# Moving the loads of v: by pairs of chunks instead of by pairs of heads, and onto GpSimd's queue

## The chip, the cores and the metric

The kernel runs on one NeuronCore of a Trainium2 chip, as one launch. The metric is the device time of one execution, in microseconds (us). Three runs of the kernel before gave 1208.64, 1209.57 and 1211.05 us, a median of 1209.57 us.

## The reference, cut to what matters

Three stages follow each other, all in float32 at their edges:

```python
# 1. attention inside chunks of 64 tokens; q, k, v are [8 batches, 8 heads, 576, 64]
scores = (q_c @ k_c.T) / 8           # per batch, head, chunk: 64 x 64
attn   = softmax(scores)
x      = (attn @ v_c)                # -> x [4608 tokens, 512]
# 2. mixture of experts: logits = x @ w_gate; tokens assigned greedily by logit,
#    at most 576 for each of 8 experts; out = relu(x @ w1[e]) @ w2[e]
# 3. h = max(x @ m1, x @ m2, x @ m3);  result = h @ m_out     [4608, 512]
```

The change touches only the loads of stage 1.

## The kernel before, in words

Attention takes the first 165 us or so of the execution. Its work is cut into nine units of 8 chunks with all 8 heads, and each unit into four groups of 2 chunks (128 tokens), 36 groups in all. `ORDER` (line 37) says what a unit is: units 0 to 3 and 5 to 8 are eight consecutive chunks of one batch; unit 4 (`None`) collects the one remaining chunk of each of the eight batches.

For a unit there are three tensors to load, 1 MB each. `load_qk` (line 52) brings q and k into a tile of 128 partitions; one DMA of 512 KB brings four heads of a whole unit in runs of 1 KB. In unit 4 every chunk comes from another batch, so there it is eight DMAs of 128 KB, each into 16 partitions; those of chunks 4 to 7 are issued by GpSimd, the others by SyncE. `load_v` (line 65) brings v into one of three buffers `VB` (`vb_93`, `vb_94`, `vb_95` in the listings below), in runs of 256 bytes. In a usual unit, part n of four holds the head pair n for all eight chunks: two DMAs of 128 KB into 64 partitions each. The first half (s = 0) is issued by SyncE, the second by GpSimd; in unit 0 both by SyncE. In unit 4 a part holds two chunks with all heads, as four DMAs of 64 KB.

The loop over groups (line 245) issues in step i the loads of coming units: of q and k one half of the heads of one of the two tensors for the unit after next (`load_qk`, unit i//4 + 2), of v part i%4 for the next unit (`load_v`, unit i//4 + 1). SyncE first issues a tiny DMA of the maxima of group i-1 (`tick`, line 249), and so its loads of step i don't start before that group's maxima exist. Then, for group i: `scores` on TensorE into the PSUM tile pS, `smax` and `ssub` on VectorE, `expo` on ScalarE. For group i-1: `att_t` transposes the weights, and `pv` multiplies by v (line 181, into pX). `pv` of a group reads chunks 2h and 2h+1 of its unit with all four head pairs in turn, 4 matmul rows for each pair. For group i-2: `scale` (line 185) divides by the row sums on VectorE and writes the tile X, and GpSimd sends X to DRAM (`xd`, line 190). X has three buffers (`bufs=3`, line 187): `scale` of group g overwrites that of group g-3, and waits until the `xd` DMA of group g-3 has landed. The transposes of q and k for the next unit (`trans`, line 105) run in the same step.

All engines run their instructions in the order in which the program issues them. DMAs signal completion through semaphores. Eight of them serve the DMAs of GpSimd in turn (DMASW0 to DMASW7) and eight those of SyncE and ScalarE (DMAHW0 to DMAHW7): the n-th DMA of a kind waits for the landing of the (n-8)-th of that kind before it is issued. So at most eight of a kind are under way.

Before the loop, SyncE issues the loads of q and k for unit 0, half of unit 1, all of v for unit 0, and the rest of unit 1. GpSimd clears two of the buffers of v (lines 91 and 92), then builds some 30 constants for the later routing stage (`consts()`, line 94), and only then comes to its part of the loop.

Of the kernel before, what the change touches and what calls it, by code (L numbers as in the profile page):

```python
# [17 lines left out]
B, H, S, D = 8, 8, 576, 64  # L18
# [10 lines left out]
def attention(ctx, tc, q, k, v, wg_in, xd, L, ident, consts, early, tick, mark):  # L29

    nc = tc.nc
# [5 lines left out]
    ORDER = [0, 1, 2, 3, None, 4, 5, 6, 7]  # L37

    def chunk(u, j):

        b = ORDER[u]
        return (b, b % 2 + j) if b is not None else (j, 0 if j % 2 else 8)
# [9 lines left out]
    def load_qk(nm, u, h, n):  # L52

        if h == 0:
            QK[nm, u] = P.tile([128, H, 4 * D], F32, name="in" + nm)
        src = k if nm == "k" else q
        m = 8 if ORDER[u] is not None else 1
        for j in range(0, 8, m):
            b, c = chunk(u, j)
            (nc.gpsimd if j >= 4 else nc.sync).dma_start(  # L60
                QK[nm, u][16 * j:16 * (j + m), h:h + n],
                bass.AP(tensor=src.tensor, offset=src.offset + (b * H + h) * S * D + c * 64 * D,
                        ap=[[4 * D, 16 * m], [S * D, n], [1, 4 * D]]))

    def load_v(u, part):

        t = VB[u % 3]
        if ORDER[u] is not None:
            b, c = chunk(u, 0)
            for s in range(2):  # L70
                (nc.gpsimd if u and s else nc.sync).dma_start(
                    t[s * 64:(s + 1) * 64, :, part, s, :],
                    bass.AP(tensor=v.tensor, offset=v.offset + (b * H + 2 * part + s) * S * D + c * 64 * D,
                            ap=[[D, 64], [64 * D, 8], [1, D]]))
            return
        for j in (2 * part, 2 * part + 1):
            b, c = chunk(u, j)
            for s in range(2):
                (nc.gpsimd if u and s else nc.sync).dma_start(
                    t[s * 64:(s + 1) * 64, j, :, s, :],  # L80
                    bass.AP(tensor=v.tensor, offset=v.offset + b * H * S * D + s * S * D + c * 64 * D,
                            ap=[[D, 64], [2 * S * D, 4], [1, D]]))

    for h in (0, 4):
        for nm in "kq":
            load_qk(nm, 0, h, 4)
# [3 lines left out]
    for t, eng in ((VB[0], nc.vector), (VB[1], nc.gpsimd), (VB[2], nc.gpsimd)):  # L90
        eng.memset(t[0:64, :, :, 1, :], 0.0)
        eng.memset(t[64:128, :, :, 0, :], 0.0)
    nc.scalar.dma_start(wg[:, :, :8], wg_in.rearrange("(a p) e -> p a e", p=128))
    consts()
    warm = PS.tile([128, 4, 128], F32, name="pA", bufs=1)
    for i in range(14):
        nc.tensor.transpose(warm[:, i % 4, :], ident, ident)
    for nm in "kq":
        load_qk(nm, 1, 0, 4)
    for n in range(4):  # L100
        load_v(0, n)
    for nm in "kq":
        load_qk(nm, 1, 4, 4)

# [140 lines left out]
    for i in range(G):  # L245
        u, n = i // 4 + 1, i % 4
# [6 lines left out]
        if tr:  # L253
            load_v(u, n)
# [440 lines left out]
def kernel(ctx, tc, q, k, v, w_gate, w1, w2, m1, m2, m3, m_out, out, mark=lambda n: None):  # L695
# [10 lines left out]
    with ExitStack() as c2:  # L706
        consts = c2.enter_context(tc.tile_pool(name="tmp", bufs=1))
        rt.unit(consts)
        attention(c2, tc, q, k, v, w_gate, xd, rt.L, rt.ident, lambda: rt.consts(consts), rt.early, tick, mark)
# [579 lines left out]
```

## Time and profile before

| quantity | value |
|---|---|
| median of 3 runs | 1209.57 us (1208.64 to 1211.05) |
| profiled execution, its own time | 1214.07 us |
| span in its profile | 1212.3 us |
| TensorE busy | 1175.5 us, 97% of the span |
| VectorE / ScalarE / GpSimd busy | 68% / 34% / 25% |
| mean granted TensorE clock | 0.985 of full speed |
| DMA | 242.99 MB, 200 GB/s on the mean |

The span runs from the first to the last instruction; the execution's own time lies 1.8 us above it. Of the page's 40 slices of 30 us the first two, the first 60 us of attention, show TensorE busy for 7 and 8 tenths, the next three for 9 tenths or more, and the DMA engines at 9 tenths or more through the first four. In the rows below, "idle" times in square brackets name what ended them; a share of DMA above 1 means that packets overlap on an engine.

### The profile page before, as it was taken

How to read it: one execution, taken by the hardware profiler on the slowest of the kernel's cores; microseconds unless marked ns; L12 is line 12 of the kernel's file. 1: busy time of each engine (PE TensorE's matmuls, PEld its weight loads, DVE VectorE, ACT ScalarE, POOL GpSimd, SP SyncE). 2: the span in 40 equal slices, each digit the busy share in tenths (PEclk: the TensorE clock that was granted, in tenths of full speed). 3: DMA queues.
4: the chain of work that ended last, by engine and by line, in shares of the span. 5: the costliest groups of instructions: out<-in, count | busy, mean ns of one | idle time of the engine just before them, and what ended most of it. 6: DMA issues, size and time to landing. Idle time of an engine off the chain costs nothing.

```text
span 1212.3 us, 23567 instructions
## 1 busy us (share of the span) xinstructions
PE 1175.5 (97%) x9508; PEld 1098.6 (91%) x9508; DVE 829.2 (68%) x1652; ACT 413.7 (34%) x674; POOL 306.8 (25%) x507
## 2 busy tenths in 40 slices
PE   7899978999999999999999999999999999999998
PEld 6788856999999999998999998998998998998996
DVE  6788976877788888787843565565565565565561
ACT  5788822333333242334432113113113113113111
POOL 7433201010027465745970002002002002002002
PEclk9999978999999999999999999999999999999999
DMA  9999615273556556567654763663763763773651
GB/s 260 246 262 263 175 54 165 89 239 116 187 171 196 190 200 215 172 226 250 222 195 181 270 243 139 269 247 136 270 250 135 270 258 128 274 258 121 230 193 52
DMA packets 138828, 242.99 MB, mean 200 GB/s; under 512 B 30048, under 2 KB 101216, under 8 KB 131808
## 3 DMA queue, kind: packets, MB, share of 16 engines
q1 hardware_dynamic: 118608, 180.90, 45.4%
q0 software_dynamic: 14976, 51.13, 12.5%
q10 hardware_dynamic: 5136, 9.46, 2.1%
q8 instruction: 75, 1.23, 0.4%
q14 instruction: 33, 0.27, 0.1%
HBM read 195.05 MB, written 46.40 MB: 199 GB/s over the span
## 4 chain that ended last, share of the span: by engine, by line
PE 50%; issue 36%; DVE 6%; DMA 4%; POOL 3%; SPq 1%; ACT 1%; POOLq 1%; DVEq 0%; ACTq 0%
PE acc L1099 16%; PE acc L1044 13%; PE pX L181 2%; PE py L1137 2%; POOL out_dram L1221 2%; PE po L1213 2%; PE pT L115 2%; PE px L1137 2%; PE pz L1137 2%; DMA inq<-in_q_dram 2%; PE pS L132 1%; PE pA L168 1%; PE pxt L816 1%; DVE chunk L763 1%; DMA vb<-in_v_dram 1%
## 5 line engine op out<-in xcount | busy, mean ns | idle before, releaser
L1044 PE MATMUL acc<-xhi,chunk 128*128 128x288 f32 (+2 forms) x1024 | 208.1, 302 | 4.8 <-DVE hlo L1077 4.1
L1099 PE MATMUL acc<-hhi,chunk 128*128 128x288 f32 x1024 | 209.9, 299 | 1.3 <-DVE hlo L1077 1.3
L1044 PEld LDWEIGHTS acc<-xhi,chunk 128*128 128x128 f32 x1024 | 161.6, 189 | 6.8 <-DVE hlo L1077 5.0
L1221 POOL DMA_INDIRECT out_dram<-ot,ia x36 | 36.4, 1012 | 516.3 <-ACT ot L1219 515.7
L1099 PEld LDWEIGHTS acc<-hhi,chunk 128*128 128x128 f32 x1024 | 162.9, 188 | 1.9 <-DVE hlo L1077 1.5
L1099 PE MATMUL acc<-hlo,chunk 128*128 128x288 f32 x512 | 150.8, 294 | 0.0
L1213 PE MATMUL po<-chunk,h 128*128 128x512 f32 x648 | 149.3, 390 | 0.0
L1213 PEld LDWEIGHTS po<-chunk,h 128*128 128x128 f32 x648 | 121.5, 188 | 24.8
L1044 PE MATMUL acc<-xlo,chunk 128*128 128x288 f32 (+2 forms) x512 | 143.8, 296 | 0.0
L1137 PE MATMUL px<-xb,wa 128*128 128x384 f32 x648 | 129.9, 334 | 0.7 <-ACT ys L1106 0.7
L1137 PE MATMUL py<-xt,wb 128*128 128x384 f32 x648 | 129.8, 334 | 0.0
L1137 PEld LDWEIGHTS px<-xb,wa 128*128 128x128 f32 x648 | 113.9, 188 | 1.4 <-ACT ys L1106 1.0
L1137 PEld LDWEIGHTS py<-xt,wb 128*128 128x128 f32 x648 | 114.0, 188 | 0.5
L1158 ACT CAST h<-best 128x384 fp32r<-128x384 f32 x72 | 37.0, 514 | 198.1 <-DVE best L1156 121.3
L1099 PEld LDWEIGHTS acc<-hlo,chunk 128*128 128x128 f32 x512 | 96.0, 188 | 0.0
L763 DVE TENSOR_TENSOR chunk<-raw,chunk 128x1024 fp32r<-128x1024 f32 x67 | 86.7, 1299 | 10.8 <-ACT chunk L756 8.0
L1044 PEld LDWEIGHTS acc<-xlo,chunk 128*128 128x128 f32 x512 | 94.1, 189 | 0.0
L1068 ACT ACTIVATE hhi<-acc 128x576 fp32r<-128x576 f32 (+1 forms) x66 | 41.9, 638 | 135.3 <-PE acc L1044 125.0
L793 POOL DMA_INDIRECT xg<-xd,idx x40 | 40.8, 1020 | 152.2 <-DVE ohe L683 75.1
L1173 ACT COPY tmp<-px 128x384 f32<-128x384 f32 x54 | 25.9, 480 | 146.2 <-PE px L1137 146.2
L756 ACT CAST chunk<-raw 128x1024 fp32r<-128x1024 f32 x67 | 69.5, 1047 | 11.3 <-ACT ys L1106 6.0
L1077 DVE SCALAR_TENSOR_TENSOR hlo<-acc,hhi 128x576 fp32r<-128x576 f32 (+1 forms) x66 | 48.3, 735 | 33.0 <-ACT hhi L1068 32.8
(221 smaller groups left out, 2048.1 us busy)
## 6 DMA issues: line engine op xcount, KB each, us to landing
wb<-wdb SPq DMA_DIRECT2D x54, 1024.0 KB
wa<-wda SPq DMA_DIRECT2D x54, 768.0 KB
raw<-in_moe_w_dram SPq DMA_DIRECT2D x64, 512.0 KB
xd<-x POOLq DMA_DIRECT2D x36, 256.0 KB
yd<-ys ACTq DMA_DIRECT2D x32, 288.0 KB
wdb<-pair POOLq DMA_DIRECT2D x18, 512.0 KB
yraw<-yd SPq DMA_DIRECT2D x12, 768.0 KB
ink<-in_k_dram SPq DMA_DIRECT2D x16, 512.0 KB
```

Source lines behind the costliest of these rows:

```text
L756: nc.scalar.copy(hi, raw)
L763: nc.vector.tensor_tensor(lo, raw, hi.bitcast(F32), op=OP.subtract)
L793: nc.gpsimd.indirect_dma_start(out=g, out_offset=None, in_=xd[:, :], in_offset=bass.IndirectOffsetOnAxis(ap=rt.idx[r][:, t:t + 1], axis=0))
L1044: nc.tensor.matmul(acc[:, hf, :tk.stop - tk.start], w[a][:, dc, o:o + 128], x[:, dc, tk], start=n == 0, stop=n == 11)
L1068: nc.scalar.activation(hv, src, AF.Relu)
L1077: nc.vector.scalar_tensor_tensor(lv, src, 0.0, hv.bitcast(F32), op0=OP.max, op1=OP.subtract)
L1099: nc.tensor.matmul(acc[:, hf, :288], w[a][:, f, :], x[:, f, tk], start=n == 0, stop=n == 23)
L1137: nc.tensor.matmul(dst, w[:, dc, o, a], XO[x][:, c, dc], start=start and n == 0, stop=stop and n == 5, skip_group_check=True)
L1158: nc.scalar.copy(hpart(g, i, j)[0], M)
L1173: nc.scalar.copy(U[g, 1], XB[g])
L1213: nc.tensor.matmul(PO[t], h[:, x, t % 6 * 128:t % 6 * 128 + 128], w[a][:, f % 2], start=f == 0 and n == 0, stop=f == 5 and n == 2)
L1221: st = nc.gpsimd.indirect_dma_start(out=out, out_offset=bass.IndirectOffsetOnAxis(ap=ia[:, t:t + 1], axis=0), in_=ot, in_offset=None)
```

## The change: what it does

1. `load_v` loses its branch for usual units. In every unit part n now holds chunks 2n and 2n+1 with all eight heads, as four DMAs of 64 KB, each of 64 partitions by four heads. That is what group n of the unit reads.
2. All v is issued by GpSimd, except part 0 of unit 0, which SyncE issues.
3. Parts 1 to 3 of unit 0 are issued by GpSimd before `consts()`; part 0 stands where all of unit 0 stood.
4. All q and k is issued by SyncE, so the 16 small DMAs of unit 4 are no longer shared between two queues.

```diff
@@ load_qk
-            (nc.gpsimd if j >= 4 else nc.sync).dma_start(
+            nc.sync.dma_start(
                 QK[nm, u][16 * j:16 * (j + m), h:h + n],
@@ load_v
         t = VB[u % 3]
-        if ORDER[u] is not None:
-            b, c = chunk(u, 0)
-            for s in range(2):
-                (nc.gpsimd if u and s else nc.sync).dma_start(
-                    t[s * 64:(s + 1) * 64, :, part, s, :],
-                    bass.AP(tensor=v.tensor, offset=v.offset + (b * H + 2 * part + s) * S * D + c * 64 * D,
-                            ap=[[D, 64], [64 * D, 8], [1, D]]))
-            return
         for j in (2 * part, 2 * part + 1):
             b, c = chunk(u, j)
             for s in range(2):
-                (nc.gpsimd if u and s else nc.sync).dma_start(
+                (nc.gpsimd if u or part else nc.sync).dma_start(
                     t[s * 64:(s + 1) * 64, j, :, s, :],
                     bass.AP(tensor=v.tensor, offset=v.offset + b * H * S * D + s * S * D + c * 64 * D,
                             ap=[[D, 64], [2 * S * D, 4], [1, D]]))
@@ before the loop
+    for n in range(1, 4):
+        load_v(0, n)
     consts()
...
     for nm in "kq":
         load_qk(nm, 1, 0, 4)
-    for n in range(4):
-        load_v(0, n)
+    load_v(0, 0)
     for nm in "kq":
         load_qk(nm, 1, 4, 4)
```

How this moves instructions is seen in three places. The first is GpSimd's queue at the start. In the kernel before, the last constants (`free` to `wsum`) are followed by v of unit 1 (`vb_94`) and the first stores of results (`xd`):

```order
L410 MEMSET free 128x36
L412 MEMSET base 128x1
L414 MEMSET wsum 128x1
L71 DMA vb_94<-in_v_dram 64x8x64 x3
L190 DMA xd<-x 128x512
L71 DMA vb_94<-in_v_dram 64x8x64
L190 DMA xd<-x 128x512
L71 DMA vb_95<-in_v_dram 64x8x64
L190 DMA xd<-x 128x512
```

In the changed kernel (line numbers are lower by 7), 12 DMAs for unit 0 (`vb_93`) stand behind the clearing of the buffers and ahead of the constants, of which the first is `lev`:

```order
L83 MEMSET vb_95 64x32x64
L84 MEMSET vb_95 64x32x64
L71 DMA vb_93<-in_v_dram 64x4x64 x12
L356 IOTA lev 128x128
L359 IOTA i_117 128x1152
```

and behind the constants 12 DMAs, no longer three, come ahead of the first `xd`, and then four between one `xd` and the next:

```order
L403 MEMSET free 128x36
L405 MEMSET base 128x1
L407 MEMSET wsum 128x1
L71 DMA vb_94<-in_v_dram 64x4x64 x12
L183 DMA xd<-x 128x512
L71 DMA vb_94<-in_v_dram 64x4x64 x4
L183 DMA xd<-x 128x512
L71 DMA vb_95<-in_v_dram 64x4x64 x4
L183 DMA xd<-x 128x512
```

So the first `xd` moved behind 21 more DMAs than before.

The second place is the same queue with its waits, from the ninth DMA for unit 1 on, in the changed kernel (DMASW is a semaphore of GpSimd's DMAs, DVE_49 one of VectorE):

```order
L71 DMA vb_94<-in_v_dram 64x4x64 [waits DMASW4_49]
L71 DMA vb_94<-in_v_dram 64x4x64 [waits DMASW5_49]
L71 DMA vb_94<-in_v_dram 64x4x64 [waits DMASW6_49]
L71 DMA vb_94<-in_v_dram 64x4x64 [waits DMASW7_49]
L183 DMA xd<-x 128x512 [waits DMASW0_49,DVE_49]
L71 DMA vb_94<-in_v_dram 64x4x64 [waits DMASW1_49]
L71 DMA vb_94<-in_v_dram 64x4x64 [waits DMASW2_49]
L71 DMA vb_94<-in_v_dram 64x4x64 [waits DMASW3_49]
L71 DMA vb_94<-in_v_dram 64x4x64 [waits DMASW4_49]
L183 DMA xd<-x 128x512 [waits DMASW5_49,DVE_49]
```

The same stretch in the kernel before has one v DMA between two stores:

```order
L190 DMA xd<-x 128x512 [waits DVE_49]
L71 DMA vb_95<-in_v_dram 64x8x64 [waits DMASW0_49]
L190 DMA xd<-x 128x512 [waits DMASW1_49,DVE_49]
L71 DMA vb_95<-in_v_dram 64x8x64 [waits DMASW2_49]
L190 DMA xd<-x 128x512 [waits DMASW3_49,DVE_49]
```

A step of the loop is now five DMAs of GpSimd where it was two, on the same eight semaphores.

The third place is SyncE's queue in steps 8 and 9, where unit 4 is loaded. Before, with four DMAs of k in step 8 and four of q in step 9:

```order
L249 DMA tick<-mx 1x1 [waits DMAHW2_49,DMAHW0_49,DVE_49]
L60 DMA ink<-in_k_dram 16x8x256 [waits DMAHW1_49,PE_49]
L60 DMA ink<-in_k_dram 16x8x256
L60 DMA ink<-in_k_dram 16x8x256 [waits DMAHW3_49]
L60 DMA ink<-in_k_dram 16x8x256 [waits DMAHW4_49]
L71 DMA vb_93<-in_v_dram 64x8x64 [waits DMAHW5_49]
L249 DMA tick<-mx 1x1 [waits DMAHW6_49,DVE_49]
L60 DMA inq<-in_q_dram 16x8x256 [waits DMAHW7_49]
```

In the changed kernel there are eight of each, and no v between them:

```order
L242 DMA tick<-mx 1x1 [waits DMAHW0_49,DVE_49]
L60 DMA ink<-in_k_dram 16x8x256 [waits DMAHW5_49,PE_49]
L60 DMA ink<-in_k_dram 16x8x256
L60 DMA ink<-in_k_dram 16x8x256 [waits DMAHW7_49]
L60 DMA ink<-in_k_dram 16x8x256
L60 DMA ink<-in_k_dram 16x8x256 [waits DMAHW1_49]
L60 DMA ink<-in_k_dram 16x8x256 [waits DMAHW2_49]
L60 DMA ink<-in_k_dram 16x8x256 [waits DMAHW3_49]
L60 DMA ink<-in_k_dram 16x8x256 [waits DMAHW4_49]
L242 DMA tick<-mx 1x1 [waits DMAHW5_49,DVE_49]
L60 DMA inq<-in_q_dram 16x8x256 [waits DMAHW6_49]
```

All of unit 4's q and k now passes through one queue in order.

## Rows read from the trace of the kernel before

**Rows 1.** Stretches by busy time of each engine, TensorE clock, DMA share.

```profile
core 0: us, PE busy (x) PEld busy (x) DVE busy (x) ACT busy (x) POOL busy (x), PEclk, DMA share, GB/s
10.90:65.53 54.63, 45.48 (x698) 37.29 (x697) 39.58 (x76) 37.49 (x65) 25.60 (x62) 0.91 1.14 249
65.53:129.38 63.85, 63.82 (x1080) 53.15 (x1079) 56.93 (x116) 57.31 (x100) 22.39 (x36) 1.00 1.03 267
58.00:63.30 5.30, 5.29 (x52) 4.53 (x52) 2.67 (x5) 1.94 (x4) 1.27 (x2) 0.50 1.09 201
```

**Rows 2.** Timeline, TensorE: start, duration, instructions, [idle before]; first products with v.

```profile
17.06 0.88 PE L181 MATMUL pX<-vb,AT 128*64 128x128 f32 x12
20.13 0.44 PE L181 MATMUL pX<-vb,AT 128*64 128x128 f32 x4 [2.19 <-DMA vb<-in_v_dram]
```

**Rows 3.** Timeline, TensorE, groups 9 to 11.

```profile
50.87 0.69 PE L132 MATMUL pS<-kT,qT 64*64 64x64 f32 x32
...
53.39 0.88 PE L181 MATMUL pX<-vb,AT 128*64 128x128 f32 x12
58.01 0.69 PE L181 MATMUL pX<-vb,AT 128*64 128x128 f32 x4 [3.74 <-DMA inq<-in_q_dram]
58.63 1.13 PE L132 MATMUL pS<-kT,qT 64*64 64x64 f32 x32
...
65.53 0.69 PE L132 MATMUL pS<-kT,qT 64*64 64x64 f32 x32
```

**Rows 4.** Timeline, SyncE's queue: issue of loads.

```profile
5.41 9.46 SPq L71 DMA_DIRECT2D vb<-in_v_dram  x8
...
42.37 2.31 SPq L71 DMA_DIRECT2D vb<-in_v_dram  x1
...
45.63 3.93 SPq L60 DMA_DIRECT2D ink<-in_k_dram  x4
```

**Rows 5.** Timeline, GpSimd: constants, loads, stores.

```profile
9.16 0.40 POOL L363 IOTA lev<- 128x128 bf16 x1
...
19.39 2.37 POOL L71 DMA_DIRECT2D vb<-in_v_dram  x3
21.75 0.59 POOL L190 DMA_DIRECT2D xd<-x  x1
...
43.67 0.57 POOL L190 DMA_DIRECT2D xd<-x  x1 [2.35 <-DMA vb<-in_v_dram]
...
51.42 0.54 POOL L60 DMA_DIRECT2D inq<-in_q_dram  x1 [1.84 <-DMA xd<-x]
```

**Rows 6.** Timeline, GpSimd, later: small loads of v, last store, and others.

```profile
66.20 1.23 POOL L79 DMA_DIRECT2D vb<-in_v_dram  x2
...
112.18 0.71 POOL L71 DMA_DIRECT2D vb<-in_v_dram  x1
...
166.14 0.54 POOL L190 DMA_DIRECT2D xd<-x  x1 [1.43 <-DVE x L188]
169.45 0.10 POOL L953 MEMSET xg<- 128x1 f32 x1 [2.77 <-PE pT L220]
```

**Rows 7.** Timeline, VectorE: scale of group 3.

```profile
35.28 0.69 DVE L188 TENSOR_TENSOR x<-pX,rc 128x512 f32<-128x512 f32 x1
```

**Rows 8.** DMA packets of 5 to 11 us (first), 51 to 55 us.

```profile
DMA packets 2103, 2.09 MB, mean 348 GB/s; under 512 B 64, under 2 KB 2103, under 8 KB 2103
...
DMA packets 442, 0.71 MB, mean 177 GB/s; under 512 B 140, under 2 KB 317, under 8 KB 442
```

**Rows 9.** DMA queues: packets, MB, share of 16 engines; 12.5 to 16.5, 151 to 167 us.

```profile
q1 hardware_dynamic: 3028, 0.75, 140.8%
...
q0 software_dynamic: 400, 1.31, 21.3%
```

**Rows 10.** One line's instructions (shortest/median/longest ns), then VectorE's timeline.

```profile
L158 DVE TENSOR_SCALAR sm<-sm x36: 140/171/678, 18.8 to 164.0; 128x8 f32<-128x8 f32 x36
...
112.57 0.32 DVE L158 TENSOR_SCALAR sm<-sm 128x8 f32<-128x8 f32 x1
```

## The prediction

> **What bounds the kernel now.** I read the stretches of the attention stage first. From the scores of group 0 at 10.90 us to those of group 11 at 65.53 us TensorE is busy for 45.48 of 54.63 us; from there to 129.38 us it is busy for 63.82 of 63.85 us [rows 1]. The second stretch holds 16 groups, so a group costs 63.85 / 16 = 3.99 us where TensorE never waits. The first holds 11 groups and would take 43.9 us at that pace: 10.7 us are lost, and the change can win back those 10.7 us and hardly more, as later groups wait for no load. In both stretches the DMA share is about 1 or above, so loads are the suspect.
>
> TensorE's timeline shows where. At 17.06 us the product of group 0 with v does 12 of its 16 rows and then idles 2.19 us for v [rows 2]. At 53.39 us group 8, the first of unit 2, again does 12 rows, idles 3.74 us and ends at 58.7 us [rows 3]. Twelve rows are three head pairs, so what is missing is part 3 of v. The row names a load of q as releaser, but such names are inferred, and this instruction reads v. SyncE issued its half of that part at 42.37 us [rows 4]: some 15 us from issue to use, although the part had been asked for only two groups ahead. After the wait the granted clock is 0.50 from 58.00 to 63.30 us [rows 1], the lower of the two levels, 1.2 GHz. So group 9 to group 10 takes 58.63 - 50.87 = 7.76 us and group 10 to group 11 takes 65.53 - 58.63 = 6.90 us [rows 3]. Against 2 x 3.99 us that is 6.7 us lost in one place.
>
> **The change part by part.** *Parts of v by groups.* Part n is now read by group n alone. A part asked for in step i is used five steps later, about 20 us at 3.99 us a step; before, part 3 had two steps, 8 us. A landing of 15 us as in rows 3 and 4 fits into 20 us and not into 8. So I let the loss of 6.7 us at group 8 go: **-6.7 us**. If landings rise above 20 us, nothing goes.
>
> *What is late next: the first stores.* The waits in the first 30 us (2.19 us among them) also become smaller, but I cost that at nothing, since another wait stands behind them. `scale` of group 3 overwrites the X of group 0 and needs the first xd to have landed; before, it starts at 35.28 us [rows 7], with its xd issued at 21.75 us [rows 5]. Now that xd stands behind 12 DMAs, the constants and 12 DMAs more. The sum: GpSimd is free at 9.16 us [rows 5]. A DMA of this shape costs 1.23 / 2 = 0.62 us of its time [rows 6]. Eight take it to 14.1 us; the ninth waits until the first has landed. For a landing I have two bounds. The last xd is issued at 166.14 us and the instruction that waits for all such landings starts at 169.45 us [rows 6], so with idle DMA engines it is at most 3.3 us. Under full load, the xd of 43.67 us gives way to the eighth DMA behind it at 51.42 us [rows 5], so about 7.7 us. With 3.3 us there is no wait, the twelfth ends at 16.6 us; with 7.7 us the ninth starts at 16.9 us and the twelfth ends at 19.4 us. I take 17.3 us, as the DMA engines are full then but hold only loads in long runs. The constants take 19.39 - 9.16 = 10.2 us [rows 5]: 27.5 us. Twelve more DMAs of 0.62 us: 34.9 us, xd. Its landing I take from the light side, 3.1 us, since by then SyncE has run out of loads that its tick allows: **38.0 us against 35.28 us, +2.7 us**, between +0.5 us (36 us) and +9.5 us (19.4 + 10.2 + 7.4 + 7.7 = 44.7 us). Behind `scale` on VectorE stand smax and ssub of group 5, for which the next scores wait, and `xT` of group 3 on TensorE. TensorE has then been idle for longer than the 3.74 us that halved its clock before. A whole group at that clock cost 6.90 - 3.99 = 2.9 us; VectorE holds part of this group back anyway, so I take half: **+1.4 us**, between 0 and 2.9 us.
>
> *GpSimd's steps.* Per step it issues four DMAs of 0.62 us and one of 0.57 us, 3.05 us of 3.99 us. Its cover is 0.94 us a step. That v is moved by GpSimd's queue costs the DMA engines less: on SyncE's queue alone 0.75 MB of v took 140.8% of 16 engines for 4 us, 8.3 KB per engine-us; on GpSimd's queue 1.31 MB of stores took 21.3% for 16 us, 24 KB per engine-us [rows 9]. No row shows v alone on GpSimd's queue; the bounds are these two, and I take the upper, as both leave in long packets. SyncE's half of a part, 131 KB, then needs 0.3 us instead of 1.0 us of all engines in a step: room, not time, for TensorE waits for no load in steady state.
>
> *One instruction of VectorE beside it.* L158 takes 171 ns in the median, 678 ns at most [rows 10]. The one at 112.57 us, beside a DMA issue of GpSimd from 112.18 to 112.89 us [rows 6], took 0.32 us. Four issues a step will often lie beside it. At 0.15 us for each of 31 steps it is 4.6 us if none of it is hidden, 0 if the issues end before; VectorE idles for 6.9 of 63.85 us [rows 1], and I take **+0.5 us**.
>
> *Unit 4 on one queue.* Its 16 DMAs of 128 KB go one behind another. The DMA engines moved 348 GB/s with loads into all partitions and 177 GB/s while unit 4 was loaded [rows 8]. SyncE starts on unit 4 at 45.63 us [rows 4], 5.2 us before group 9; all of it is needed three groups after group 9, and 1 us later for the transposes: 5.2 + 12.0 + 1.0 = 18.2 us. Needed: 2.1 MB at 177 GB/s, 11.9 us, and 4.5 groups of v and xd, 0.52 MB each, at 267 GB/s, 8.8 us, less 4.5 x 0.65 us saved on v: 17.8 us. That is level. Bounds: 0, and +5 us if the two queues' side-by-side work was what gave 177 GB/s. I take **+1.0 us**.
>
> Sum: -6.7 + 2.7 + 1.4 + 0.5 + 1.0 = -1.1 us. The profiled execution took 1214.07 us, 4.5 us above the median of the runs; as all terms lie in one stage and none is scaled by the rest, I set the sum against the median as it stands: 1209.57 - 1.1 = 1208.5 us (1213.0 us for the profiled one).
>
> **The rivals.** *The early wait is short.* If v lands in 3.3 us, the issues stay at 0.62 us or less and xd lands 2 us after its issue, `scale` starts near 36 us; the clock falls for half the time, and unit 4 comes in time: -6.7 + 0.7 + 0.7 = -5.3 us, 1204.3 us. For it: the DMA engines lose 0.7 us a step of work. Against it: 24 issues and 10.2 us of constants can't end before 34.2 us.
>
> *Unit 4 becomes the wait (slower).* Place: TensorE's transposes of step 12. Eight DMAs into 16 partitions each, in order, use an eighth of the partitions at a time; before, two queues filled two such sets. If that halves the pace of unit 4 below what rows 8 show, it lands 5 us late instead of 1 us: -1.1 + 4.0 = +2.9 us, 1212.5 us. It decides when unit 4 needs more than the 18.2 us above. For it: 177 against 348 GB/s. Against it: fewer other packets share the engines. The Trainium skill, SBUF — State Buffer, section Door 1: The DMA port swizzle, says that bandwidth goes by how many of 16 ports the partitions reach, 27.2 GB/s each; 16 partitions in a row reach four, so by that page, as an estimate, 109 GB/s and 19.3 us for unit 4, which is this rival. The trace agrees as far as it goes: the mean fell to half with two sets in flight.
>
> *The first landings are slow (slower).* With 7.7 us landings at the start `scale` waits until 42 us or more: +3 us, 1212.6 us. Against it: by 28 us SyncE's loads of units 0 to 2, 6.3 MB at 348 GB/s, are done.
>
> *GpSimd sets the pace (slower).* Eight DMAs under way and five a step: the step is five eighths of a landing, above 3.99 us once a landing exceeds 6.4 us. At 7.7 us it is 4.8 us; the store's three steps of slack absorb some, and ten steps' worth of 0.85 us would remain: +8 us, 1217.5 us. For it: landings near 7.7 us before 58 us. Against it: less work for the DMA engines.
>
> **How the numbers follow.** A difference of 0.2%, 2.4 us, is what a measurement here can tell from none. Chances: forecast 0.45 (1206 to 1211 us), short early wait 0.27, unit 4 0.14, slow landings 0.08, GpSimd's pace 0.06. Faster by over 2.4 us: most of the short wait and 0.13 of the forecast, 0.37. Slower: most of the three slower rivals and 0.03 of the forecast, 0.26. Within: 0.37. The range 1203.5 to 1215 us holds all cases but GpSimd's pace and the ends.
>
> **What would show it.** In the profile after: no wait of `pv` for v at the first group of a unit; `scale` of group 3 idle until a landing of xd near 38 us, with TensorE idle some 7 us before it and a granted clock of 0.5 behind; GpSimd's constants from 17 to 28 us; group 11 near 63 us; v on GpSimd's queue in packets of some KB. Wrong if `scale` waits again at later groups, if group 12's transposes wait for q by more than 2 us, or if a group takes more than 4.1 us after 70 us.

## The result, and the profile after

The changed kernel took 1218.99 us, the median of 6 runs (1217.84 to 1220.79), against 1210.73 us for the kernel before in 6 runs beside it (1208.64 to 1212.52): a ratio of 1.0070, 95% interval 1.0056 to 1.0085. It is slower by 8.3 us, and lies 4 us above the upper end of my range. The profiled execution took 1218.49 us, with a span of 1216.4 us.

I read the stretches of the attention stage first. The columns are those of [rows 1]. Kernel after:

```profile
30.00:40.00 10.00, 2.75 (x58) 2.27 (x52) 1.86 (x5) 3.46 (x7) 9.72 (x17) 0.79 0.61 173
40.16:46.00 5.84, 5.84 (x61) 5.06 (x62) 5.22 (x10) 2.41 (x4) 5.66 (x10) 0.50 0.85 221
2.00:70.00 68.00, 53.05 (x786) 43.89 (x785) 45.85 (x83) 43.57 (x75) 54.02 (x102) 0.92 0.96 233
87.48:135.50 48.02, 48.02 (x816) 39.98 (x816) 43.19 (x89) 43.08 (x76) 37.92 (x64) 1.00 0.96 272
```

And two of the same stretches of the kernel before:

```profile
30.00:40.00 10.00, 9.65 (x181) 8.36 (x176) 9.00 (x19) 9.05 (x17) 2.53 (x4) 1.00 1.17 246
2.00:70.00 68.00, 57.55 (x831) 47.53 (x831) 49.76 (x91) 46.42 (x80) 36.08 (x72) 0.92 1.12 259
```

From 87 us on TensorE is busy without a gap, as it was before: the loss lies ahead of that. Between 30 and 40 us TensorE works for 2.75 us instead of 9.65, and the DMA engines, which had a share of 1.17, have 0.61. Hold on to the last number of the rows that begin at 2.00: 233 against 259 GB/s, over 68 us 15.8 against 17.6 MB.

Who waits in the hole is seen on VectorE. The timeline of `scale` (groups 3, 5, 8, 9 and 11), kernel after, answers [rows 7]; in brackets the idle time and what ended it:

```profile
39.32 0.69 DVE L181 TENSOR_TENSOR x<-pX,rc 128x512 f32<-128x512 f32 x1 [8.03 <-DMA xd<-x]
48.42 0.69 DVE L181 TENSOR_TENSOR x<-pX,rc 128x512 f32<-128x512 f32 x1
64.66 0.69 DVE L181 TENSOR_TENSOR x<-pX,rc 128x512 f32<-128x512 f32 x1 [3.60 <-DMA xd<-x]
70.26 0.69 DVE L181 TENSOR_TENSOR x<-pX,rc 128x512 f32<-128x512 f32 x1 [2.08 <-PE pT L108]
80.31 0.69 DVE L181 TENSOR_TENSOR x<-pX,rc 128x512 f32<-128x512 f32 x1 [2.24 <-DMA xd<-x]
```

Groups 3, 8 and 11 wait for the landing of a store. So does group 9 by the program, for the store of group 6: the row names a transpose as releaser, but `scale` reads nothing of it. The first wait is the one that I had forecast, at 39.3 us instead of 38.0; the later ones I had given to a rival, and they are one of the signs that I had named for being wrong. The stores are GpSimd's; its timeline after answers [rows 5]:

```profile
18.89 0.40 POOL L356 IOTA lev<- 128x128 bf16 x1
29.13 5.61 POOL L71 DMA_DIRECT2D vb<-in_v_dram  x9
35.02 1.84 POOL L71 DMA_DIRECT2D vb<-in_v_dram  x3 [0.28 <-DMA vb<-in_v_dram]
36.84 0.57 POOL L183 DMA_DIRECT2D xd<-x  x1
...
50.10 0.62 POOL L71 DMA_DIRECT2D vb<-in_v_dram  x1
52.50 0.61 POOL L71 DMA_DIRECT2D vb<-in_v_dram  x1 [1.78 <-DMA vb<-in_v_dram]
53.95 0.61 POOL L71 DMA_DIRECT2D vb<-in_v_dram  x1 [0.84 <-DMA xd<-x]
54.76 0.62 POOL L71 DMA_DIRECT2D vb<-in_v_dram  x1 [0.20 <-issue]
55.73 0.56 POOL L183 DMA_DIRECT2D xd<-x  x1 [0.35 <-DVE sm L149]
```

The constants begin at 18.9 us and end at 29.1; 12 loads follow, and the first xd leaves at 36.84 us. The last five rows are a later store in full. Group 5's X is written by 49.11 us (the row at 48.42). Ahead of its store stand four loads of v, which wait 1.78 + 0.84 us for earlier ones to land; the store leaves at 55.73 us, 6.6 us late, and lands 8.9 us later, when `scale` of group 8 starts at 64.66 us. That is 15.5 us where three buffers allow three steps, 12 us. TensorE and SyncE, kernel after, in that order of fences (answering [rows 3] and [rows 4]; the second is SyncE's queue):

```profile
40.16 1.09 PE L192 MATMUL pY<-ident,x 128*128 128x128 f32 x4 [7.41 <-DVE x L181]
59.23 1.09 PE L174 MATMUL pX<-vb,AT 128*64 128x128 f32 x16
64.59 0.49 PE L108 MATMUL pT<-ident,inq 128*128 128x128 f32 x3 [2.95 <-issue]
```

```profile
28.81 0.39 SPq L60 DMA_DIRECT2D inq<-in_q_dram  x1
40.91 0.40 SPq L60 DMA_DIRECT2D ink<-in_k_dram  x1
51.12 3.66 SPq L60 DMA_DIRECT2D ink<-in_k_dram  x8
```

The product of group 8 at 59.23 us runs its 16 rows in one go: the wait of [rows 3] for part 3 of v is gone. But TensorE stood for 7.41 us before 40.16 us, and SyncE issued no load between 28.81 and 40.91 us, because each load stands behind the tick of the group before it. Unit 4's loads start at 51.12 us; in [rows 4] they started at 45.63 us. The idle time at 64.59 us has no releaser. It ends together with VectorE's wait of 3.60 us for a store, so this profile can't tell which of the two held the stage; the last section comes back to it.

### The profile page after: what moved, and what is told of

It reads as the page before. It is cut to its first block, busy times and chain, and to the rows that moved or that the text cites. A ratio compares the mean times of both kernels' runs of the same rounds, so it can differ in the third digit from the quotient of the medians.

```text
span 1216.4 us, 23678 instructions
## 1 busy us (share of the span) xinstructions
PE 1173.3 (96%) x9508; PEld 1096.0 (90%) x9508; DVE 826.8 (68%) x1652; ACT 412.6 (34%) x674; POOL 359.8 (30%) x603
## 3 DMA queue, kind: packets, MB, share of 16 engines
q10 hardware_dynamic: 5136, 9.46, 2.1%
## 4 chain that ended last, share of the span: by engine, by line
PE 50%; issue 37%; DVE 6%; POOL 5%; DMA 2%; POOLq 1%; ACT 1%; SPq 0%; DVEq 0%; ACTq 0%
PE acc L1092 16%; PE acc L1037 13%; PE pX L174 3%; PE py L1130 2%; POOL out_dram L1214 2%; PE pT L108 2%; PE px L1130 2%; PE pz L1130 2%; PE pS L125 2%; PE pA L161 1%; DVE chunk L756 1%; PE pxt L809 1%; PE po L1206 1%; PE pY L192 1%; POOL vb L71 1%
## 5 line engine op out<-in xcount | busy, mean ns | idle before, releaser
L71 POOL DMA_DIRECT2D vb<-in_v_dram x140 | 86.1, 624 | 25.8 <-DMA vb<-in_v_dram 11.9
L749 ACT CAST chunk<-raw 128x1024 fp32r<-128x1024 f32 x67 | 69.5, 1047 | 10.6 <-ACT ys L1099 6.0
```

The costliest lines, as they stand in the source:

```text
L71: (nc.gpsimd if u or part else nc.sync).dma_start(t[s * 64:(s + 1) * 64, j, :, s, :], bass.AP(tensor=v.tensor, offset=v.offset + b * H * S ...
L749: nc.scalar.copy(hi, raw)
```

## The experiments

Each was timed beside the kernel before, whose median was 1209.8 to 1211.1 us; three were single executions with a profile. "Group 5" and so on is the start of that group's `smax` in the timeline. The theories: A, two separate losses (the first store behind 24 loads and the constants; unit 4 on one queue); B, five GpSimd DMAs a step on eight semaphores are the loss wherever they stand; C, the loads are late and the stores only show it; P, on the profile of before; D, formed after fifteen runs, on the DMA engines being what is short.

**Parts undone.** e1 undoes parts 2 and 3 of the change for unit 0, e2 undoes part 4, e3 both.

```diff
e1: -  (nc.gpsimd if u or part else nc.sync).dma_start(   # load_v
    +  (nc.gpsimd if u else nc.sync).dma_start(
    -  for n in range(1, 4): load_v(0, n)                 # ahead of consts()
    -  load_v(0, 0)
    +  for n in range(4): load_v(0, n)
e2: -  nc.sync.dma_start(                                 # load_qk
    +  (nc.gpsimd if j >= 4 else nc.sync).dma_start(
```

e1: 

> The changed kernel, but with all of v for unit 0 on SyncE's queue at its old place and nothing ahead of the constants on GpSimd. Theory A (two separate losses: the first store of results behind 24 loads and the constants, and unit 4 on one queue): scale of group 3 starts near 33 us instead of 39.3 us, the clock stays up, groups 8 to 12 still wait for stores; about 1213 us against 1219 us. Theory B (five DMAs of GpSimd per step on eight semaphores are the loss wherever they stand): the early gain is given back at groups 8 to 12, about 1218 us.

e2: 

> The changed kernel, but with the loads of q and k for chunks 4 to 7 of unit 4 on GpSimd's queue again. Theory A: unit 4 lands sooner, landings on GpSimd's queue fall below 8 us, and the waits of scale for stores in groups 8 to 12 (8.2 us idle in the profile) mostly go; about 1213 us, scale of group 3 unchanged near 39 us. Theory B: GpSimd has even more DMAs in steps 8 and 9, nine each; the waits stay or grow, 1219 to 1222 us.

e3: 

> Both of these undone: v of unit 0 on SyncE, unit 4 on two queues; what is left of the change is v by chunks and on GpSimd from unit 1 on. Theory A: 1207 to 1209 us, below the kernel before by the 3.7 us wait for v and its slow clock. Theory B: 1216 us or more.

Measured: e1 1215.2 us, ratio 1.0042 (1.0025 to 1.0060); e2 1221.36 us, 1.0088 (1.0068 to 1.0107); e3 1215.2 us, 1.0044 (1.0029 to 1.0059). e2 came out as theory B said, e1 between the two, e3 near B. Sharing unit 4 between two queues is not faster than after (1.0070, the intervals overlap), so unit 4's single queue is not the loss. In e2 TensorE waits for a result that waits for its store, here for group 10; TensorE, kernel e2:

```profile
77.40 0.84 PE L192 MATMUL pY<-ident,x 128*128 128x128 f32 x3 [3.85 <-DVE x L181]
```

e1 trades one early wait for another, and no `scale` of it waits for a store, though GpSimd has five DMAs a step from unit 1 on, as in after. SyncE's queue and then TensorE, kernel e1:

```profile
5.16 14.62 SPq L71 DMA_DIRECT2D vb<-in_v_dram  x16
20.47 0.51 SPq L60 DMA_DIRECT2D inq<-in_q_dram  x1
```

```profile
27.22 1.09 PE L107 MATMUL pT<-ident,inq 128*128 128x128 f32 x4 [8.12 <-DMA inq<-in_q_dram]
```

Sixteen DMAs of 64 KB, behind the loads of q and k, take 14.6 us to issue, with eight under way at most; q of unit 1 leaves at 20.5 us, and TensorE waits 8.12 us for it. In [rows 4] eight of 128 KB stood there and took 9.46 us.

**More buffers of X.** e4 is after, e8 before, each with `bufs=6` instead of 3 for `x`.

e4: 

> The changed kernel with six buffers instead of three for the results X, so that scale overwrites what was stored six groups earlier. Theory A and B both put the loss into scale waiting for stores: all four waits (14.2 us idle in the profile) go, 1207 to 1210 us. Theory C (the loads of v or of unit 4 themselves are late, and the stores only show it): the waits turn into waits of TensorE for v or q, 1215 us or more.

e8: 

> The control of e4: the kernel before with six buffers of X instead of three. Theories B and A: before has no wait of scale for a store that matters, so its time stays: ratio 0.999 to 1.001, and the 7 us that six buffers gave in e4 are what the change had lost. Rival: the buffers are worth as much without the change, so before gains as well: ratio 0.995 or less, and e4 then says little of the change.

Measured: e4 1211.8 us, 1.0007 (0.9990 to 1.0023); e8 1211.41 us, 1.0012 (0.9997 to 1.0026). e4 came out above the range of A and B and below that of C. Before gains nothing, after gains 7 us: the waits of `scale` for stores carry nearly all of the loss. In e4's profile this gain lies at the first store: group 9 starts at 50.6 us, 7.4 us earlier than in after, but from there to group 16 e4 takes 34.0 us, after 34.7. Other waits of TensorE stand there in e4, 2.8 us without a releaser and 1.26 us at the transposes of unit 4. So with the waits for stores gone the change is worth nothing either.

**Queues and counts.** e5 is before with v by chunks, its queues untouched; e6 is after with v of units 1 to 8 (not unit 4) in the old pairs of heads, so three DMAs a step on GpSimd instead of five; e7 is after with the stores on SyncE; e11 is after with each load of v from unit 1 on cut in two.

```diff
e5: -  if ORDER[u] is not None: ...; return               # load_v of before
e6: +  if u and ORDER[u] is not None:                     # load_v of after
    +      (two nc.gpsimd.dma_start of 64x8x64, as before); return
e7: -  nc.gpsimd.dma_start(xd[...], X[g]...)
    +  nc.sync.dma_start(xd[...], X[g]...)
e11:+  for p in range(0, 4, 2): (dma_start of t[..., j, p:p + 2, s, :])
```

e5: 

> The kernel before with one part of the change alone: v by single chunks of four heads, on the queues of before (SyncE one half, GpSimd the other, unit 0 all on SyncE, no v ahead of the constants; unit 4 shared). GpSimd then has three DMAs a step instead of five. Theory B (five GpSimd DMAs a step on eight semaphores make the stores late): no wait of scale for a store after group 5; the wait for v at group 8 is gone (-6.7 us against before), but the 16 DMAs of 64 KB of unit 0 on SyncE take about 14.6 us to issue, as in e1, and group 3 waits for q of unit 1 (+4 us): 1206 to 1208 us, ratio 0.997 to 0.999. Theory C (small loads are late wherever they stand): SyncE now has four DMAs a step and its loads are late in turn, TensorE waits for q or k after 40 us: 1213 us or more, ratio above 1.003.

e6: 

> The kernel after with the v of units 1 to 8, but for unit 4, by pairs of heads as before (two DMAs of 128 KB a step), all on GpSimd. The bytes on GpSimd's queue stay as in after, the DMAs per step fall from five to three. Theory B (the number of DMAs on eight semaphores): the stores are in time again at groups 9 and 10, the loss that stays is the first store behind the constants (about +4 us) and a wait for part 3 of v at group 8 as in before; in unit 4's own steps, where five a step stay, a wait is left: 1211 to 1214 us, ratio 1.001 to 1.004. Theory C (the bytes on GpSimd's queue, or late loads): as after or worse, as the wait for part 3 comes back on top: 1219 us or more, ratio above 1.007.

e7: 

> The kernel after with the stores of X issued by SyncE instead of GpSimd; GpSimd keeps its four loads of v a step. Theory B: the loss is that a store stands behind loads of v in one in-order queue. With the store on the other queue scale no longer waits at groups 3 to 5 and 9 to 12, most of the 8 us goes: 1208 to 1212 us, ratio 0.998 to 1.002; a wait may be left where the store stands behind the eight small DMAs of unit 4 on SyncE. Theory C (the loads of v themselves are late, the stores only show it): pv waits for v instead, time stays at 1216 us or more, ratio above 1.005.

e11: 

> The kernel after with each load of v from unit 1 on cut in two (two heads, 32 KB): eight of them and a store, nine DMAs a step on GpSimd, the bytes unchanged. Theory B (number of DMAs on eight semaphores): a step takes nine eighths of a landing, 6 us at landings of 5.5 us, and GpSimd's issues alone take 3 to 5 us a step; scale waits for stores far into the stage: 1230 us or more, ratio above 1.016. Theory C (bytes): the queue moves the same bytes, time within 3 us of after's 1219 us.

Measured: e5 1217.84 us, 1.0058 (1.0036 to 1.0079); e6 1214.72 us, 1.0033 (1.0016 to 1.0049); e7 1215.22 us, 1.0037 (1.0023 to 1.0051); e11 1279.9 us, 1.0557 (1.0531 to 1.0582). e5 missed: no `scale` waits for a store, but the wait of e1 is there (8.12 us at 27.35 us). e6 came out close to theory B and shows what the number of DMAs does and does not do. VectorE, `scale` of groups 3 and 9, then GpSimd, the store of group 9, kernel e6:

```profile
39.11 0.69 DVE L189 TENSOR_TENSOR x<-pX,rc 128x512 f32<-128x512 f32 x1 [7.76 <-DMA xd<-x]
64.65 0.69 DVE L189 TENSOR_TENSOR x<-pX,rc 128x512 f32<-128x512 f32 x1
```

```profile
65.64 0.57 POOL L191 DMA_DIRECT2D xd<-x  x1 [0.78 <-DVE x L189]
```

With three DMAs a step the store leaves as soon as its X is written, and none is waited for after group 3, but the wait at group 3 stays. e7 came out just below the bound of theory C. Its stores no longer stand behind loads of v; now `pv` of group 4 waits for v of unit 1, which GpSimd issues behind unit 0 and the constants, and `scale` of group 10 waits 3.98 us for a store, on SyncE's queue with unit 4. TensorE, kernel e7:

```profile
34.98 1.94 PE L174 MATMUL pX<-vb,AT 128*64 128x128 f32 x16 [2.15 <-DMA vb<-in_v_dram]
```

e11 lets GpSimd set the pace throughout. Waits from 10 to 170 us (us in total, times, longest) and GpSimd's timeline, kernel e11:

```profile
DVE x L183 <- DMA xd<-x: 67.5, 17, 15.0
```

```profile
43.84 4.81 POOL L73 DMA_DIRECT2D vb<-in_v_dram  x8
48.48 0.73 POOL L185 DMA_DIRECT2D xd<-x  x1
```

A DMA of 32 KB costs GpSimd 0.60 us, as much as one of 64 KB; nine a step are over 5 us of issuing alone, and 17 stores are waited for up to 170 us, 25 in the whole stage. The eight loads leave one behind another: here the issuing is the limit, not the landings, so e11 tests the number of DMAs, but not that eight are under way at most.

**The two kernels, profiled again.** e9 and e15 are before, e10 is after, all unchanged.

e9: 

> The kernel before, unchanged, profiled a second time. Its first profile ran 1214.07 us, above nearly all of its other runs (1207 to 1214 us, median 1210.5). Theory P: the wait of 3.74 us for part 3 of v at group 8 and the slow clock behind it, 6.7 us in that profile, are larger there than in a usual execution, so part of what I wanted to win was never in the median: here group 9 to group 11 takes under 12 us instead of 14.7 us, and the run 1208 to 1211 us. Rival: the wait is as long in every execution (group 9 to group 11 14 us or more), and the profile was late for another reason.

e10: 

> The changed kernel, unchanged, profiled a second time. Theory B: the waits of scale for the store stand at the same groups: one of over 6 us at group 3, and together over 5 us at groups 7 to 11; run 1217 to 1221 us. Rival: the waits behind group 3 vary from execution to execution and are not what makes the kernel slow; here they are under 2 us together.

e15: 

> The kernel before, a third profile. Theory P (the wait at group 8 is not in every execution): the stretch from group 9 to group 11 takes under 9.5 us again, as in e9 (8.8 us), and the run about 1208 to 1211 us. Rival (e9 was the odd one): 14 us, run above 1212 us.

Measured: 1208.75 us (e9), 1220.17 us (e10), 1208.75 us (e15). TensorE at the product of group 8, first e9, then e15, beside the 12 and 4 rows of [rows 3] with 3.74 us between them:

```profile
53.90 1.09 PE L181 MATMUL pX<-vb,AT 128*64 128x128 f32 x16
```

```profile
52.83 0.88 PE L181 MATMUL pX<-vb,AT 128*64 128x128 f32 x12
56.38 0.48 PE L181 MATMUL pX<-vb,AT 128*64 128x128 f32 x4 [2.68 <-DMA inq<-in_q_dram]
```

In e9 there is no wait, in e15 one of 2.68 us. From group 9 to group 11 the three profiles of before take 14.4, 8.8 and 12.2 us, where 8.0 us would be no loss: 6.4, 0.8 and 4.2 us, 3.8 us on the mean. So theory P holds, though e15 came out between its two numbers. e10 repeats after: 8.56 us at group 3, 2.93 and 4.11 us at groups 8 and 10.

**The gathered unit later.** e12 is e4 with unit 4 as unit 6.

```diff
-    ORDER = [0, 1, 2, 3, None, 4, 5, 6, 7]
+    ORDER = [0, 1, 2, 3, 4, 5, None, 6, 7]
```

> The kernel after with six buffers of X, as in e4, and with the gathered unit as unit 6 instead of unit 4 (its order among the units, nothing else). Theory B with the view that the first 65 us are short of loads and what comes later is not: unit 4 then is a usual one, and the waits of 6.5, 6.5 and 6.6 us at groups 10 to 13 of e4 shrink to 4 us each (-5 us); by unit 6 the loads are no longer behind, so its 16 small DMAs cost at most 2 us: 1206 to 1209 us, ratio 0.996 to 0.999. Rival: the gathered unit costs the same wherever it stands: 1211 to 1213 us, ratio 1.000 to 1.002.

Measured: 1210.95 us, 1.0002 (0.9988 to 1.0016), near the rival's number. The waits near 60 us are gone, and a new one stands where unit 6 is transposed; TensorE, kernel e12:

```profile
100.21 1.08 PE L108 MATMUL pT<-ident,inq 128*128 128x128 f32 x4 [2.58 <-DMA tick<-mx]
```

**The first unit alone, and the constants moved.** e13 is before with v of unit 0 as in the change (parts 1 to 3 on GpSimd ahead of the constants), e14 is e13 with six buffers of X. e16 is after with six buffers and `consts()` in step 16; e17 is e16 with the order of e12; e18 is e14 with `consts()` in step 16.

```diff
e13: ...                                        # load_v(0, n): as in the change
     +  for n in range(1, 4): load_v(0, n)      # GpSimd
        consts()
     ...
     -  for n in range(4): load_v(0, n)
     +  load_v(0, 0)                            # SyncE
e16: -  consts()                                # ahead of the loop
     +  if i == 16: consts()                    # in the loop, behind load_v
```

e13: 

> The kernel before with one part of the change alone: v of unit 0 by chunks, parts 1 to 3 issued by GpSimd ahead of the constants, part 0 by SyncE; all later loads as before, so that GpSimd has two DMAs a step, not five. Theory B: the waits for v and q in the first groups go as in the changed kernel (group 5 would start 4 us earlier than in before), the first store stands behind 12 + 3 loads and lands near 33.5 us instead of 39.3 us, so scale of group 3 waits about 2 us and group 5 starts near 34 us against 35.9 and 36.7 us; no wait for stores behind it: 1207 to 1210 us, ratio 0.997 to 1.000. Theory A (the first store behind the constants is the loss): scale of group 3 waits 6 us or more, 1214 us or more, ratio above 1.003.

e14: 

> As the one before, with six buffers of X, so that the first store is waited for three groups later. Theory B: group 5 starts near 32 us (as in e4), nothing takes that back before unit 4, attention ends at 152 to 155 us: 1203 to 1207 us, ratio 0.994 to 0.997, faster than both kernels. Rival (the loads as a whole are late, and a group won at the start is lost at unit 4, as in e8 and e4): 1210 to 1212 us, ratio 0.999 to 1.001.

e16: 

> The kernel after with six buffers of X and the 30 constants moved from ahead of the loop into step 16. Theory D (formed from the runs so far: in the first 70 us the DMA engines are what is short; GpSimd issues nothing for 10 us while it builds constants, and while TensorE waits SyncE's loads wait for the tick, so every early wait comes back at unit 4): v of unit 1 and the first stores leave 10 us earlier, the waits of 5.7 and 4.5 us at groups 5 to 7 of e4 go, more has been moved by 40 us, unit 4's waits shrink, and the constants cost at most 2 us later, where stores have six buffers and v five steps: 1206 to 1209 us, ratio 0.996 to 0.999. Theory B alone (five DMAs a step are the loss): stores and loads are as late behind group 5 as in e4 and 10 us more at step 16: 1212 us or more.

e17: 

> As the one before, with the gathered unit as unit 6, as in e12. Theory D: no load that matters is late before 80 us, and the wait of 7.5 us at group 20 of e12 stays or shrinks: 1203 to 1207 us, ratio 0.993 to 0.997. Rival: the constants in step 16 push the stores and v into the loading of the gathered unit, and it waits longer than in e12: 1211 us or more, ratio above 1.000.

e18: 

> The kernel before with the first unit's loads as in the change, six buffers of X (as in e14), and the constants in step 16. Theory D: the wait for v of unit 1 at group 6 (10.0 us in e14) goes, as GpSimd issues its half 10 us earlier; two DMAs a step on GpSimd leave room for the constants: 1204 to 1208 us, ratio 0.994 to 0.998, faster than both kernels. Rival (the half of v in runs of 256 bytes on SyncE's queue is what delays all loads in e14): the wait at group 6 stays, 1213 us or more, ratio above 1.002.

Measured: e13 1215.75 us, 1.0038 (1.0025 to 1.0050); e14 1216.16 us, 1.0036 (1.0017 to 1.0055); e16 1209.89 us, 0.9998 (0.9985 to 1.0011); e17 1208.44 us, 0.9986 (0.9972 to 1.0001); e18 1211.77 us, 1.0018 (1.0002 to 1.0033).

e13 came out as theory A said, where B had put 1207 to 1210 us. GpSimd has two DMAs a step and the loss is half there. GpSimd and VectorE, kernel e13:

```profile
31.18 0.61 POOL L191 DMA_DIRECT2D xd<-x  x1
```

```profile
40.00 0.69 DVE L189 TENSOR_TENSOR x<-pX,rc 128x512 f32<-128x512 f32 x1 [9.23 <-DMA xd<-x]
```

The first store leaves 5.7 us earlier than in after and is waited for just as long: 8.8 us from issue to use, against 2.5 us in after (36.84 to 39.32). In that time SyncE's queue, with v in its 256-byte packets, holds the engines (share by queue from 31 to 36 us, packets and MB ahead of it, under a line on the sizes of all packets, kernel e13):

```profile
DMA packets 1238, 1.08 MB, mean 216 GB/s; under 512 B 597, under 2 KB 1145, under 8 KB 1237
...
q1 hardware_dynamic: 1103, 0.69, 79.2%
q0 software_dynamic: 134, 0.38, 35.1%
```

e14 missed both of its numbers; e18 lies between its two, nearer the rival. In both v of unit 1 is late instead: the product of group 4 waits 3.05 us, then 1.61 us more, in e14, where GpSimd issues its half from 29.4 us on, behind the constants. In e18 that half leaves from 19.0 us on and the product still waits 3.07 us: SyncE's half of part 2, whose issue ends at 29.3 us, was the late one. e16 has all parts of the change and no early wait; its stretches and SyncE's first load of unit 4:

```profile
30.00:40.00 10.00, 10.00 (x182) 8.28 (x181) 9.35 (x20) 9.16 (x16) 7.09 (x12) 1.00 1.08 288
2.00:70.00 68.00, 62.57 (x992) 52.53 (x993) 58.29 (x109) 55.01 (x95) 48.86 (x73) 1.00 1.07 272
```

```profile
40.23 5.08 SPq L60 DMA_DIRECT2D ink<-in_k_dram  x8
```

The five DMAs a step are the same as in after, and with six buffers they cost little that is seen: `scale` waits once for a store, 2.69 us at group 20, behind the constants. With three buffers this was not tried. But the gain that theory D promised did not come either: e16 is at 0.9998 where D had 0.996 to 0.999, e17 a little above its range, and against e4, e16 moved 30 GB/s more by 70 us and is 1.9 us faster, with intervals that overlap. e16's profile has attention end (last `smax`) at 154.3 us, against 160.3, 156.5 and 157.7 us in the three of before and 166.5 and 168.1 us in the two of after. But over 12 runs e16 only equals before, and e17's interval still touches 1. No version is shown to beat the kernel before.

**All together.** What the DMA engines moved from 2 to 70 us (from the stretches, in the one profiled execution of each), and the median time:

| kernel | GB/s, 2 to 70 us | time, us |
|---|---|---|
| e17, e16 | 281, 272 | 1208.4, 1209.9 |
| before, three profiles | 259, 271, 271 | 1210.7 |
| e18, e8, e12 | 268, 259, 262 | 1211.8, 1211.4, 1211.0 |
| e6, e7 | 251, 251 | 1214.7, 1215.2 |
| e1, e5, e14 | 248, 247, 247 | 1215.2, 1217.8, 1216.2 |
| e3, e13 | 242, 238 | 1215.2, 1215.8 |
| e2 | 235 | 1221.4 |
| after, two profiles | 233, 228 | 1219.0 |
| e11 | 195 | 1279.9 |
| e4 | 242 | 1211.8 |

But for e4, a kernel that had moved less by 70 us took longer, give or take 3 us. That is an order and no proof: a kernel that waits also loads less, since its ticks come late, and e4 and e16 show that the bytes alone decide little.

## Why the prediction was wrong, point by point

I take the starts of `smax` on the mean of the three profiles of before, and in the first of after: group 5 at 36.0 and 39.9 us, group 9 at 51.9 and 58.0, group 16 at 84.0 and 92.7, the last group at 158.2 and 166.5. The last pair differs by 8.4 us, about as much as the medians (8.3). These come as +3.9 us up to group 5, +2.1 to group 9, +2.6 to group 16 and -0.2 behind it.

- *Parts of v by groups, -6.7 us.* The mechanism held: no product waits for v at group 8 any more. The size was wrong. I took it from one execution, 3.3 us above the median of its kernel, and set it against the median; three profiles show 6.4, 0.8 and 4.2 us, on the mean 3.8. So 2.9 us of the gain were not there to be had.
- *The first stores, +2.7 and +1.4 us.* Place, cause and clock were right: constants from 18.9 to 29.1 us (forecast 17 to 28), TensorE idle for 7.41 us (some 7), granted clock 0.50 behind it from 40.16 to 46.00 us. Up to group 9 after loses 6.0 us where these terms give 4.1, inside their bounds. That is most of the 8.3 us. e6 and e13, which have this wait and wait for no store behind it, are 1.0033 and 1.0038 of before; e4, which has no such wait, reaches group 9 at 50.6 us.
- *The step that failed: "GpSimd's steps ... Its cover is 0.94 us a step", for which I put nothing.* From group 9 to 16 after loses 2.6 us against before, though the 3.8 us of the wait for v are gone: 6.4 us are new. The cover is not there. From the timelines, how long after its X is written a store of groups 3 to 15 leaves, and how long groups 9 to 16 take:

| kernel | GpSimd's DMAs a step | store leaves after X, us | group 9 to 16, us |
|---|---|---|---|
| before, three profiles | 2 (more in steps 8 and 9) | 0.3 to 0.5; up to 4.6 at groups 7 and 8 | 34.7, 29.3, 32.4 |
| e13 | 2 (more in steps 8 and 9) | 0.3; up to 3.3 at groups 7 and 8 | 34.3 |
| e6 | 3 (5 in steps 12 to 15) | 0.3 to 1.2 | 29.1 |
| e1 | 5 | 2.3 to 5.6 | 30.5 |
| e3 | 5 (more in steps 8 and 9) | 3.5 to 10.8 | 32.6 |
| after, two profiles | 5 | 4.1 to 9.3, 2.1 to 9.6 | 34.7, 35.3 |
| e2 | 5 (more in steps 8 and 9) | 1.2 to 12.8 | 35.1 |
| e4 (six buffers) | 5 | 11.7 to 19.3 | 34.0 |

  The 0.94 us is a sum of issue times and leaves out that the issue waits for a landing eight DMAs back. With five a step, landings of 8.9 us make a step of 5.6 us, and after's stores of groups 3 to 8 leave 5.6 us apart on the mean (46.57 to 74.67 us). I had this as a rival, with 6.4 us as the point from which it decides and 1217.5 us as its time, and gave it 0.06, because v would leave SyncE's short packets and the engines would have less to do. The engines are full all the same when unit 4 is loaded, as the rows on shares below show. That the rival's time is near the measured one is in part luck: most of the loss lies ahead of group 9.

  What the late stores cost is shown in part only. In after VectorE waits some 8 us for them at groups 8 to 11; TensorE idles 2.4 us behind these waits, and 2.95 us without a releaser while VectorE's longest wait runs. In e2 and e3, without such an idle time, TensorE waits 5.0 and 2.9 us for X alone, and in e6 there is hardly any of either. Against it: e1 has five a step, its stores leave late, and `scale` still waits for none, so five a step alone are not enough; and e4, without these waits, is no faster than after from group 9 to 16.
- *Unit 4 on one queue, +1.0 us.* No transposes of steps 12 to 15 wait for its q or k in after, and e2, with two queues, is no faster: the term is nil there, and the rival that rested on it fell. Where no store holds the stage, as in e4, the transposes of step 12 do wait, for 1.26 us. What I missed is what else is in flight then. In before it was part 3 of v that came late, in after it is the stores.
- The rate that this rival rested on was right. SyncE's queue, which carried little but unit 4 from 54 to 60 us, moved 0.68 MB, 113 GB/s, at nearly the full share of the engines. By queue, packets, MB and share, kernel after:

```profile
q1 hardware_dynamic: 750, 0.68, 95.5%
q0 software_dynamic: 72, 0.16, 16.6%
```

  The Trainium skill, SBUF — State Buffer, section Door 1: The DMA port swizzle, gave, as an estimate, 109 GB/s for loads into 16 partitions; the trace agrees within 4%.
- *L158 beside GpSimd's issues, +0.5 us.* Behind group 16 after is not slower than before, so nothing of it is seen.

Open: e13 has two DMAs a step and no `scale` that waits for a store behind group 3, and takes as long from group 9 to 16 as after (34.3 and 34.7 us). There TensorE idles 4.4 us without a releaser (last section); what makes it start was not separated. So how the 6.4 us divide between the stores and this idle time stays open. Nor was it tried whether e16 keeps its time with three buffers.

## What to carry to other kernels

The capacity of a queue has two limits. One is the sum of its issue times, as in e11. The other, with so many DMAs under way at most, is that number over the landing time, and the landing to take is that of the busiest stretch, not of the quiet one. How long a store may be late is set by the buffers behind it. A wait that one execution shows, above all one that runs over its kernel's median, is worth a second profile before it is counted as a gain. And what is taken off a crowded stretch at one place can come late at another: before pricing a removed wait, list what else is in flight there and how many buffers it has.

## What the runs showed of the hardware that I had not expected

- DMAs of 64 KB on SyncE's queue, 16 in a row with eight under way at most, did not keep the engines busy. In e1, once the q and k ahead of them had been moved, the queue moved 0.47 MB from 14 to 20 us, 78 GB/s; with DMAs of 128 KB it moved 0.75 MB in 4 us [rows 9]. By queue, packets, MB and share, kernel e1:

```profile
q1 hardware_dynamic: 1943, 0.47, 35.4%
```

- The same store of 256 KB took 2.5 us from issue to use with the engines at a share of 0.59 (after) and 8.8 us at 1.12, beside packets of 256 bytes (e13).
- One kernel's runs spread by up to 9 us (e4, 1205.92 to 1214.70 us), and waits of 0 to 3.7 us for the same load in three executions of before show one thing that such a spread can come from.
- TensorE can idle in the midst of one set of matmuls. In after, e4, e10 and e13 among others it stops inside the transposes of step 10 or after 20 or 23 of the 32 scores of step 12, for 1.9 to 3.0 us and with no releaser. Each time a packet of a queue of instructions moves while it stands. But such packets come some 5 to 12 us apart here in nearly all kernels, and in the first profile of before none of them meets such an idle time. TensorE, kernel e10, and the queues from 71.1 to 72.6 us, kernel e13, whose scores resume at 73.85 us after 2.50 us:

```profile
64.88 0.49 PE L108 MATMUL pT<-ident,inq 128*128 128x128 f32 x3 [1.92 <-issue]
75.79 0.45 PE L125 MATMUL pS<-kT,qT 64*64 64x64 f32 x12 [2.27 <-issue]
```

```profile
q0 software_dynamic: 110, 0.35, 74.3%
q1 hardware_dynamic: 335, 0.08, 36.9%
q8 instruction: 1, 0.02, 5.7%
```

  From 69.5 to 71.1 us that queue had no packet. So TensorE's own program may come late when loads fill the engines. That it waits for this packet is argued from the times alone; no run here tested it.
